# Score matmuls cut into 32 weight columns, other planned transfer lengths, and loads of a DRAM tile placed behind its last store

## The chip, the core and the metric

One NeuronCore of a Trainium2 chip runs the whole program. The metric is the device time of one execution in microseconds. The engines are PE (TensorE: matmuls and transposes; its weight loads, PEld, run beside them), DVE (VectorE), ACT (ScalarE), POOL (GpSimd) and SP (SyncE, which here only issues DMAs). Each engine runs its own instructions in the order in which the program emitted them, and waits on semaphores for the others.

## The reference

Three stages in a row, all in float32. B = 8 batches, H = 8 heads, S = 576 tokens, D = 64, 32 packed queries per head.

```python
def sm_attn(qq, kk, vv):                      # softmax attention, scale 1/sqrt(64)
    s = scale * np.matmul(qq, kk.transpose(0, 1, 3, 2))
    ...
    return np.matmul(a, vv)
p_packed = sm_attn(p, k, v)                   # 32 packed rows per head
x = sm_attn(q, p_packed, p_packed)            # every token against the 32 rows
x = x.transpose(0, 2, 1, 3).reshape(4608, 512)

expert_idx = np.argmax(xn @ en.T / tau, 1)    # 8 experts, one for each token
out[mask] = gate_w[mask, None] * (np.maximum(x[mask] @ w1[e], 0) @ w2[e])

a = x @ w_a;  b = x @ w_b                     # x is now the output of the experts
return a * b @ w_out                          # 512 -> 1536 -> 512
```

## The kernel before, in words

**Attention** (up to about 210 us). `prep(b)` loads p, k (two halves of four heads, 0.59 MB each) and v (1.18 MB; two halves for batch 0) of one batch, transposes k, computes the scores of the 32 packed rows and multiplies them with v. `query(u)` treats one of 18 units of 256 tokens: 128 partitions of two tokens each. It loads q (line 423), transposes it (433), and `s2_mm` (447) multiplies it, for each head, with the packed rows ppT of the token's batch. What follows in `rest` is a softmax on DVE and ACT, a transpose (501), the product with the packed rows (512) and the store of x to a DRAM tile (537).

In `s2_mm` the 128 columns of a unit are the weight side of the matmul. `pieces(sg, most)` cuts them: a piece is 32, 64 or 128 columns, at most `most`, starts at a multiple of its own size and stays inside one batch. Batches are 288 of these columns long, so four units (2, 6, 11 and 15) are cut between two batches at column 32 or 96. With `most` = 64 they fall into pieces of 32, 32 and 64 columns, and all others into two pieces of 64. A unit has two groups of four heads: so there are 8 groups of 4 x 3 matmuls ("mixed" below) and 28 groups of 4 x 2 ("even" below). The trace shows each float32 matmul as two instructions.

**Routing.** As soon as 25 of the 36 tiles of x are there, DVE ranks the tokens by expert (the function of line 784 and the steps recorded at line 685), and POOL gathers the rows of x for the first experts' slots while the last units of attention still run.

**Experts** (about 213 to 661 us): 16 slots of 288 tokens. A slot has four groups of 24 `up` matmuls and four of 24 `dn` matmuls (lines 1038 to 1040). Its weights are loaded by SP (line 1178) into raw tiles, and ACT and DVE split each into a high and a low part (1338, 1340). ACT issues two stores for each slot (line 1267) that put the transposed result into a DRAM tile, `x2T`. Beside the slots, SP loads, and DVE and ACT convert, the weights of the last stage (1069 to 1099), and `before` (line 1583 ff.) prepares the first pair of token halves for it: nine loads of 0.39 MB from `x2T` (line 1596), sums on DVE (1568), and a split on ACT (1575) and DVE (1578).

**Last stage** (to the end): a loop of matmuls for w_a, w_b and w_out.

**What sets the order.** All of this is given as operations to a planner, `Sched`. An operation has a planned length on the engines that may do it, a priority, the operations that it needs, and the buffers that it takes and frees. `run` picks, again and again, the operation that can start first by the plan (of those within 0.05 us of it the one of lowest priority), and emits it. So the planned lengths and priorities set only the order of the instructions on each engine; the chip waits for real semaphores. DMAs planned on "D" are issued by SP in that order. A load of `x2T` on the chip waits for every store to `x2T` that was emitted before it, whichever rows it reads.

Of the kernel before, what the change touches and what calls it, by code (L numbers as in the profile page):

```python
# [18 lines left out]
B, H, S, D, NP, E = 8, 8, 576, 64, 32, 8  # L19
# [52 lines left out]
class Sched:  # L72
# [14 lines left out]
        self.sizes, self.taken = sizes, {p: [] for p in sizes}  # L87
        self.ops = []

    def op(self, engs, fn, deps=(), prio=0.0, take=(), free=(), lat=None, bias={}, start=0.0, after=None):  # L90


        o = self.Op()
        o.engs, o.fn, o.deps, o.prio, o.take, o.free = engs, fn, [d for d in deps if d], prio, take, free
        o.lat, o.end, o.bias, o.start, o.after = self.LAT if lat is None else lat, None, bias, start, after
        for b in free:
            b.need += 1
        self.ops.append(o)
        return o

    def run(self, most=None, **clock):


        todo = list(self.ops)
        while todo:
            cand = []
            for n, o in enumerate(todo[:most]):
                if any(d.end is None for d in o.deps) or o.after and o.after.end is None:
                    continue
                ready, ok = {None: o.start}, True  # L110
                for i, b in enumerate(o.take):
                    t = self.taken[b.pool]
                    at = len(t) - self.sizes[b.pool] + sum(b2.pool == b.pool for b2 in o.take[:i])
                    if at >= 0:
                        old = t[at]
                        ok = ok and old.need == 0
                        ready[None] = max(ready.get(None, 0.0), old.at + self.LAT)
                if not ok:
                    continue
                best = None  # L120
                for e, dur in o.engs.items():
                    at = max([clock.get(e, 0.0), ready.get(None, 0.0)]
                             + [d.end + (self.SAME if d.eng == e and d.lat <= self.LAT else d.lat) for d in o.deps])
                    key = at + dur + o.bias.get(e, 0.0)
                    if best is None or key < best[0]:
                        best = (key, at, dur, e)
                cand.append((best[1:], n, o))
            assert cand, "no operation can go"
            t0 = min(x[0][0] for x in cand)
            (at, dur, e), n, o = min((x for x in cand if x[0][0] <= t0 + self.EPS),  # L130
                                     key=lambda x: (x[2].prio, x[0][0], x[1]))
            todo.pop(n)
            o.eng, o.end = e, at + dur
            if e != "none":
                clock[e] = o.end
            for b in o.take:
                self.taken[b.pool].append(b)
            for b in o.free:
                b.need -= 1
                b.at = max(b.at, o.end)  # L140
            o.fn(e)
        return clock


def attention(ctx, tc, c, q, k, v, p, x_dram, consts, more):
# [28 lines left out]
    op, Buf = S_.op, Sched.Buf  # L174
# [26 lines left out]
    def pieces(sg, most):  # L201

        for b, _, n, o in sg:
            end = o + n
            while o < end:
                m = max(x for x in (32, 64, 128) if x <= most and o % x == 0 and o + x <= end)
                yield b, o, m
                o += m
# [5 lines left out]
    ppT_ops, ppx_ops = {}, {}  # L214

    def prep(b):
        ahead = AHEAD
        lo, hi = (first[b - 1] - ahead, first[b] - ahead) if b else (-8.0, -1.0)
        at = lambda f: lo + (hi - lo) * f
# [6 lines left out]
        def load(n, x, h0, n_h):  # L226
            def f(e):
                if n == "k":
                    tile_("k", ("k", b, h0 // 4), [CW, 4, CI, D])
                    out = T_["k", b, h0 // 4]  # L230
                else:
                    if h0 == 0:
                        tile_(n, (n, b), [CW, H, CI, D])
                    out = T_[n, b][:, h0:h0 + n_h]
                nc.sync.dma_start(out=out, in_=x[b, h0:h0 + n_h].rearrange("h (p i) d -> p h i d", i=CI))
            return f

        o_p = op({"D": 0.2}, load_p, prio=at(-1.0), take=[bp], lat=2.0)
        o_k, o_v = [], []
        for n, x, l, pr, n_h in (("k", k, o_k, -1.0, 4), ("v", v, o_v, -0.6, 4 if b == 0 else H)):  # L240
            for h in range(0, H, n_h):
                l += [op({"D": 3.3 * n_h / H}, load(n, x, h, n_h), deps=l[-1:], prio=at(pr) + 0.01 * h,
                         take=[bk[h // 4]] if n == "k" else [] if h else [bv], lat=2.0)] * n_h


# [13 lines left out]
        o = op({"T": 0.44}, pT_mm, deps=[o_p], prio=at(0), take=[t, bpT], free=[bp])  # L259
# [16 lines left out]
        for h in range(H):  # L276
            t = Buf("tr")
            bkT.append(Buf(f"kT{h}"))
            o = op({"T": 0.25}, kT_mm(h), deps=[o_k[h]], prio=at(0.03 * h), take=[t, bkT[h]], free=[bk[h // 4]])
            o_kT.append(op({"A": 0.3, "V": 0.36}, kT_ev(h), deps=[o], prio=at(0.03 * h), free=[t]))  # L280

        for g in range(2):
# [97 lines left out]
            f = lambda x, g=g: at(x + 0.17 * g)  # L380
            be, beT, bs = Buf("e"), Buf("eT"), Buf("sm")
            evs = []
            for h in range(2):
                t = Buf("tr")
                o = op({"T": 0.56}, s1_mm(h), deps=[o_pT] + o_kT[4 * g:4 * g + 4], prio=f(0.2), take=[t] if h else [t, be],
                       free=[bpT] + bkT[4 * g:4 * g + 4])
                evs.append(op({"A": 0.3, "V": 0.36}, s1_ev(h), deps=[o] + evs, prio=f(0.2),
                              free=[t]))
            o = op({"V": 0.86}, mx, deps=evs, prio=f(0.3))
# [25 lines left out]
    def query(u):  # L415

        sg = segs(u)
        bs = [b for (b, _, _, _) in sg]

        def load(e):  # L420
            tile_("q", ("q", u), [128, H, 2 * D])
            for (b, col, n, o) in sg:
                nc.sync.dma_start(out=T_["q", u][o:o + n],
                                  in_=q[b, :, col:col + 2 * n, :].rearrange("h (p r) d -> p h (r d)", r=2))


        def qT_mm(g):
            def f(e):
                ps = psum("tr", ("qTp", u, g))
                if g == 0:  # L430
                    tile_("qT", ("qT", u), [128, H, 128])
                for j in range(4):
                    nc.tensor.transpose(ps[:, j * 128:(j + 1) * 128], T_["q", u][:, 4 * g + j, :], c.ident)
            return f

        def qT_ev(g):
            return lambda e: copy(e, T_["qT", u][:, 4 * g:4 * g + 4],
                                  T_["qTp", u, g].rearrange("p (i q) -> p i q", i=4))

        def s2_mm(g):  # L440
            def f(e):
                if g == 0:
                    psum("sm", ("s2", u))
                for j in range(4):
                    h = 4 * g + j
                    for b, o, n in pieces(sg, 64):
                        nc.tensor.matmul(
                            T_["s2", u][o:o + n, h * 64:h * 64 + 64], lhsT=T_["qT", u][:, h, o:o + n],
                            rhs=T_["ppT", b, g][:, j].rearrange("p r k -> p (r k)"), start=True, stop=True)
            return f  # L450

        B_ = {n: Buf(n) for n in ("q", "qT", "sm")}
        o = op({"D": 1.46}, load, prio=2 * u - 3.5, take=[B_["q"]], lat=2.0)
        qs, ss = [], []
        for g in range(2):
            tr = Buf("tr")
            o_q = op({"T": 0.44}, qT_mm(g), deps=[o] + qs, prio=2 * u - QA, take=[tr] + ([] if g else [B_["qT"]]),
                     free=[B_["q"]])
            qs.append(op({"A": 0.47, "V": 0.6}, qT_ev(g), deps=[o_q], prio=2 * u - QA, free=[tr]))
        for g in range(2):  # L460
            ss.append(op({"T": 0.61}, s2_mm(g), deps=[qs[g]] + [d for b in bs for d in ppT_ops[b, g]] + ss,
                         prio=2 * u, take=[] if g else [B_["sm"]],
                         free=[B_["qT"]] + [T_["bppT", b, g] for b in bs]))
        for r in range(2):
            rest(u, r, sg, bs, ss, B_["sm"])

    def rest(u, r, sg, bs, ss, sm):
# [92 lines left out]
        o_sq = op({"A": 0.62}, sq, deps=[o], prio=f(1.5), take=[B_["sq"]], free=[B_["sq"], B_["xs"]])  # L560
        o_d = op({"P": 0.17}, dots, deps=[o], prio=f(1.5), free=[B_["xs"]])
        o_r = op({"P": 0.55}, root, deps=[o_sq], prio=f(1.5))
        o_s = op({"D": 0.73}, store, deps=[o], prio=f(1.0), free=[B_["xs"]], lat=2.0)
        x_ops[t] = (o_r, o_d, o_s)

    for b in range(B):
# [918 lines left out]
class Moe2:  # L1485
# [96 lines left out]
    def before(self, S, pool, conv, stores, y, n, routed, raw):  # L1582


        D, op, Buf, HB = self.nc.sync, S.op, S.Buf, self.HB
        ys = [y[s, i] for s in range(-(-2 * HB // SLOT)) for i in (1, 3)]
        q_at, o_q, b_q = {}, {}, {}

        def load(key, p, tag, bufs):
            b_q[key], st = Buf(tag), {}  # L1590
            q_at[key] = st

            def f(e):
                st["t"] = pool.tile([128, 2, HB], F32, tag=tag, name="xq64", bufs=bufs)
                r0, t0 = key[0] * 256, key[1] * HB
                D.dma_start(out=st["t"], in_=self.x2T[r0:r0 + 256, t0:t0 + HB].rearrange("(k p) t -> p k t", p=128))

            o_q[key] = op({"D": 1.1}, f, deps=ys, prio=p, take=[b_q[key]], lat=2.0)

        p = n - 2.6  # L1600
        order = dict((name, parts) for name, _, parts in self.ORDER)
# [512 lines left out]
```

## Time and profile before

| | us |
|---|---|
| median of 3 runs | 1511.3 (1503.77 to 1513.59) |
| the profiled execution | 1511.94 |
| its span, first to last instruction | 1510.2 |
| PE busy | 1467.4 (97% of the span) |
| DVE, ACT, POOL busy | 946.4, 741.2, 169.9 |
| DMA | 276.15 MB, 183 GB/s over the span |

The profiled execution took 0.64 us longer than the median, and 1.7 us of it lie outside its span. Busy time of PE is the union of its matmuls, with modelled ends; PEclk is the TensorE clock that was granted, as a share of full speed.

### The profile page before, as it was taken

What the parts mean: (1) busy time and instruction counts of PE and PEld (TensorE: products, weight loads), DVE (VectorE), ACT (ScalarE), POOL (GpSimd) and SP (SyncE); (2) the same over time, 40 slices, a digit from 0 to 9 for tenths busy, and PEclk for the clock granted to TensorE, in tenths of its full rate; (3) what the DMA queues carried; (4) which work ended last, traced back from release to release, by engine and by line L of the source; (5) the groups of instructions that cost most, each with busy time, mean ns of one, the idle gap of its engine ahead of it and who ended that gap; (6) DMA issues with size and microseconds to landing.
All of it is one profiled execution on the core that took longest, in us unless ns stands there. A gap on an engine that the chain in (4) does not pass through costs nothing.

```text
span 1510.2 us, 27918 instructions
## 1 busy us (share of the span) xinstructions
PE 1467.4 (97%) x10257; PEld 1341.2 (89%) x10257; DVE 946.4 (63%) x1954; ACT 741.2 (49%) x1530; POOL 169.9 (11%) x274
## 2 busy tenths in 40 slices
PE   6999988999999999999999999999999999999997
PEld 4667668999999999989999999999999999999996
DVE  3566789998899886638886535544464365343442
ACT  4677766466666665535555333433443253333332
POOL 1333350120111101100002000100010010001001
PEclk9999999999999999999999999999999999999998
DMA  9788461284777866247777555755665575556551
GB/s 239 198 221 219 125 195 46 63 239 137 230 210 234 256 188 199 81 144 244 272 255 253 161 161 158 241 159 156 204 204 160 157 240 162 161 153 207 162 154 63
DMA packets 199121, 276.15 MB, mean 183 GB/s; under 512 B 16664, under 2 KB 116248, under 8 KB 198976
## 3 DMA queue, kind: packets, MB, share of 16 engines
q1 hardware_dynamic: 183776, 244.76, 54.4%
q0 software_dynamic: 6336, 20.06, 4.0%
q10 hardware_dynamic: 8864, 9.46, 1.8%
q8 instruction: 84, 1.38, 0.4%
q14 instruction: 61, 0.50, 0.1%
HBM read 256.39 MB, written 59.77 MB: 209 GB/s over the span
## 4 chain that ended last, share of the span: by engine, by line
issue 37%; PE 17%; POOL 1%; DMA 1%; ACT 0%; POOLq 0%; ACTq 0%
PE o L1929 2%; PE o L1928 2%; PE o L1930 2%; PE pa L1040 2%; PE pb L1040 2%; PE pb L1039 2%; PE pa L1039 2%; PE pb L1038 2%; PE pa L1038 2%; POOL out_dram L1952 1%; DMA out_dram<-osb,idxu 1%; ACT osb L1947 0%; ACT s L1815 0%; POOL mark L1951 0%; ACT xq L1726 0%
## 5 line engine op out<-in xcount | busy, mean ns | idle before, releaser
L1679 DVE TENSOR_TENSOR s<-s,s 128x384 f32<-128x384 f32 x324 | 176.5, 555 | 325.3 <-ACT s L1815 323.0
L1038 PE MATMUL pa<-xq,wq 128*128 128x384 f32 x504 | 169.9, 337 | 3.4 <-PEq L1468 1.8
L1038 PE MATMUL pb<-xq,wq 128*128 128x384 f32 x504 | 170.2, 338 | 1.0 <-DVE s L1679 0.7
L1928 PE MATMUL o<-oh,gh 128*128 128x512 f32 x432 | 170.3, 394 | 0.8 <-ACT osb L1947 0.8
L1040 PE MATMUL pa<-xq,wq 128*128 128x384 f32 x504 | 170.6, 339 | 0.0
L1039 PE MATMUL pb<-xq,wq 128*128 128x384 f32 x504 | 170.4, 338 | 0.0
L1040 PE MATMUL pb<-xq,wq 128*128 128x384 f32 x504 | 170.4, 338 | 0.0
L1929 PE MATMUL o<-ol,gh 128*128 128x512 f32 x432 | 170.4, 394 | 0.0
L1930 PE MATMUL o<-oh,gl 128*128 128x512 f32 x432 | 170.3, 394 | 0.0
L1039 PE MATMUL pa<-xq,wq 128*128 128x384 f32 x504 | 170.2, 338 | 0.0
L1815 ACT COPY s<-pa 128x384 f32<-128x384 f32 x180 | 86.6, 481 | 152.8 <-PE pa L1040 152.6
L1038 PE MATMUL up<-xh,w1h 128*128 128x288 f32 x512 | 153.3, 299 | 4.6 <-DVE hl L1239 4.0
L1815 ACT COPY s<-pb 128x384 f32<-128x384 f32 x180 | 86.7, 482 | 143.4 <-PE pb L1040 143.3
L1038 PE MATMUL dn<-hh,w2h 128*128 128x288 f32 x512 | 155.0, 303 | 0.0
L1039 PE MATMUL up<-xl,w1h 128*128 128x288 f32 x512 | 152.3, 297 | 0.3 <-DVE xl L1313 0.3
L1040 PE MATMUL up<-xh,w1l 128*128 128x288 f32 x512 | 151.8, 296 | 0.0
L1039 PE MATMUL dn<-hl,w2h 128*128 128x288 f32 x512 | 151.7, 296 | 0.0
L1040 PE MATMUL dn<-hh,w2l 128*128 128x288 f32 x512 | 151.5, 296 | 0.0
L1952 POOL DMA_INDIRECT out_dram<-osb,idxu x30 | 32.3, 1078 | 683.7 <-ACT osb L1947 683.3
L1038 PEld LDWEIGHTS pa<-xq,wq 128*128 128x128 f32 x504 | 95.0, 188 | 12.0 <-DVE s L1679 2.2
L1038 PEld LDWEIGHTS pb<-xq,wq 128*128 128x128 f32 x504 | 94.9, 188 | 10.5 <-DVE s L1679 1.0
L1039 PEld LDWEIGHTS pb<-xq,wq 128*128 128x128 f32 x504 | 94.8, 188 | 8.4
(265 smaller groups left out, 3143.5 us busy)
## 6 DMA issues: line engine op xcount, KB each, us to landing
wq<-ws SPq DMA_DIRECT2D x420, 256.0 KB
raw<-in_moe_w_dram SPq DMA_DIRECT2D x128, 512.0 KB
ws<-wq SPq DMA_DIRECT2D x84, 256.0 KB
k<-in_k_dram SPq DMA_DIRECT2D x16, 576.0 KB
x_dram<-xs SPq DMA_DIRECT2D x36, 256.0 KB
x2T<-y ACTq DMA_DIRECT2D x32, 288.0 KB
v<-in_v_dram SPq DMA_DIRECT2D x7, 1152.0 KB
xr<-x2T SPq DMA_DIRECT2D x20, 384.0 KB
```

The lines of the kernel that those rows point to most:

```text
L1038: nc.tensor.matmul(ps, lhsT=wh, rhs=xh, start=start, stop=False, **kw)
L1039: nc.tensor.matmul(ps, lhsT=wh, rhs=xl, start=False, stop=False, **kw)
L1040: nc.tensor.matmul(ps, lhsT=wl, rhs=xh, start=False, stop=stop, **kw)
L1679: VT = lambda out, a, b, o: V.tensor_tensor(out=out, in0=a, in1=b, op=o)
L1815: A.copy(out=T[n, key], in_=ps[n, names_bank[key]])
L1928: nc.tensor.matmul(a, lhsT=gh[:, h, s], rhs=wh, start=first, stop=False)
L1929: nc.tensor.matmul(a, lhsT=gh[:, h, s], rhs=wl, start=False, stop=False)
L1930: nc.tensor.matmul(a, lhsT=gl[:, h, s], rhs=wh, start=False, stop=last)
L1952: i = nc.gpsimd.indirect_dma_start(out=self.out, out_offset=IOA(ap=c.idxu[:, q:q + 1], axis=0), in_=st["o"], in_offset=None)
```

## The change

It does three things. `s2_mm` cuts the weight columns into pieces of at most 32 instead of 64, for all 18 units: 16 matmuls for each group of four heads, instead of 12 or 8, with 0.58 instead of 0.61 us in the plan. The planned lengths of attention's transfers go up by about 30% (k and v 3.3 to 4.2 for eight heads, q 1.46 to 1.9, the store of x .73 to .95), and the priorities of the k and v loads of a batch go up, that is later: from -1.0 and -0.6 to -0.75 and -0.45 of a batch's stretch. And the planner gets a rule: an operation can be given others that it comes `behind`, and then starts in the plan no sooner than `land` after the end of those of them that are placed already. The nine loads of `x2T` come behind the stores of odd index, two of a slot's four, with land = 7.0, and their planned length goes from 1.1 to 1.5. No work is added but the cut, and none is taken away; line numbers in the changed file are 4 higher after line 130 and 5 higher in `before`.

```diff
-    def op(self, engs, fn, deps=(), prio=0.0, take=(), free=(), lat=None, bias={}, start=0.0, after=None):
+    def op(self, engs, fn, deps=(), prio=0.0, take=(), free=(), lat=None, bias={}, start=0.0, after=None,
+           behind=(), land=0.0):
...
+        o.behind, o.land = behind, land
...
                 if not ok:
                     continue
+                ready[None] = max([ready[None]] + [d.end + o.land for d in o.behind if d.end is not None])
...
-        for n, x, l, pr, n_h in (("k", k, o_k, -1.0, 4), ("v", v, o_v, -0.6, 4 if b == 0 else H)):
+        for n, x, l, pr, n_h in (("k", k, o_k, -0.75, 4), ("v", v, o_v, -0.45, 4 if b == 0 else H)):
             for h in range(0, H, n_h):
-                l += [op({"D": 3.3 * n_h / H}, load(n, x, h, n_h), deps=l[-1:], prio=at(pr) + 0.01 * h,
+                l += [op({"D": 4.2 * n_h / H}, load(n, x, h, n_h), deps=l[-1:], prio=at(pr) + 0.01 * h,
...
-                    for b, o, n in pieces(sg, 64):
+                    for b, o, n in pieces(sg, 32):
...
-        o = op({"D": 1.46}, load, prio=2 * u - 3.5, take=[B_["q"]], lat=2.0)
+        o = op({"D": 1.9}, load, prio=2 * u - 3.5, take=[B_["q"]], lat=2.0)
...
-            ss.append(op({"T": 0.61}, s2_mm(g), ...
+            ss.append(op({"T": 0.58}, s2_mm(g), ...
...
-        o_s = op({"D": 0.73}, store, deps=[o], prio=f(1.0), free=[B_["xs"]], lat=2.0)
+        o_s = op({"D": 0.95}, store, deps=[o], prio=f(1.0), free=[B_["xs"]], lat=2.0)
...
         ys = [y[s, i] for s in range(-(-2 * HB // SLOT)) for i in (1, 3)]
+        out = [o for (_, i), o in y.items() if i % 2]
...
-            o_q[key] = op({"D": 1.1}, f, deps=ys, prio=p, take=[b_q[key]], lat=2.0)
+            o_q[key] = op({"D": 1.5}, f, deps=ys, prio=p, take=[b_q[key]], lat=2.0, behind=out, land=7.0)
```

Since the planner sees other lengths, the order of the whole of attention moves. Three places follow.

The first is PE's order at unit 2, which lies across batches 0 and 1 (ppT_190 and ppT_191 are their packed rows, sm the scores in PSUM). Before:

```order
L512 MATMUL x<-ppx_549,aT 128x264
L447 MATMUL sm<-ppT_190,qT 32x64
L447 MATMUL sm<-ppT_191,qT 32x64
L447 MATMUL sm<-ppT_191,qT 64x64
L447 MATMUL sm<-ppT_190,qT 32x64
```

And of the change:

```order
L451 MATMUL sm<-ppT_190,qT 32x64
L451 MATMUL sm<-ppT_191,qT 32x64 x3
L451 MATMUL sm<-ppT_190,qT 32x64
L451 MATMUL sm<-ppT_191,qT 32x64 x3
L516 MATMUL x<-ppx_421,aT 128x264
```

The piece of 64 columns became two of 32, and each head now has four pieces of one shape.

The second place is PE's order in the first expert slots, at the second ranking (O is the one-hot of the experts, xt a PSUM tile; ACT copies what the matmul with the ones has written there, before the matmul with the triangle `low` comes). Before:

```order
L1040 MATMUL up_3726<-xh,w1l_93 128x288
L784 LDWEIGHTS ones
L784 MATMUL xt_3729<-O,ones 128x288
L1212 MATMUL xt_3730<-ident,xg_81 128x96
L1212 MATMUL xt_3730<-ident,xg_82 128x96
L1212 MATMUL xt_3730<-ident,xg_83 128x96
L784 LDWEIGHTS low
L784 MATMUL xt_3729<-O,low 128x288
L1038 MATMUL dn_3727<-hh_3715,w2h_3707 128x288
```

And of the change:

```order
L788 LDWEIGHTS ones
L788 MATMUL xt_3985<-O,ones 128x288
L1216 MATMUL xt_3986<-ident,xg_81 128x96
L1216 MATMUL xt_3986<-ident,xg_82 128x96
L1216 MATMUL xt_3986<-ident,xg_83 128x96
L1042 MATMUL up_3982<-xh,w1h_92 128x288
L1043 MATMUL up_3982<-xl,w1h_92 128x288
L1044 MATMUL up_3982<-xh,w1l_93 128x288
```

A whole group of 24 `up` matmuls, up_3982, stands now between the two matmuls of the ranking; `low` comes after it.

The third place is SP's order near the end of the experts, with the loads of `x2T` (xq) between the loads of the experts' weights (raw). Before:

```order
L1178 DMA raw_3703<-in_moe_w_dram 128x8x128
L1596 DMA xq_8052<-x2T 128x2x384
L1178 ISA
L1178 DMA raw_3704<-in_moe_w_dram 128x8x128
L1178 ISA
L1178 DMA raw_3705<-in_moe_w_dram 128x8x128
L1178 ISA
L1178 DMA raw_3706<-in_moe_w_dram 128x8x128
L1099 DMA wb_63<-ca 128x512
L1596 DMA xq_8158<-x2T 128x2x384
L1596 DMA xq_8186<-x2T 128x2x384
```

And of the change:

```order
L1182 DMA raw_3961<-in_moe_w_dram 128x8x128
L1182 ISA
L1182 DMA raw_3962<-in_moe_w_dram 128x8x128
L1601 DMA xq_8779<-x2T 128x2x384
L1601 DMA xq_8782<-x2T 128x2x384
L1601 DMA xq_8826<-x2T 128x2x384
L1601 DMA xq_8856<-x2T 128x2x384
L1601 DMA xq_8901<-x2T 128x2x384
L1601 DMA xq_9055<-x2T 128x2x384
L1472 COMPARE_AND_BRANCH
```

Six of the nine loads now stand behind the last load of expert weights, with nothing but a branch behind them.

## Rows read from the trace of the kernel before

**Rows 1.** The page: busy time of PE, and the granted clock in 40 slices.

```profile
PE 1467.4 (97%) x10257; PEld 1341.2 (89%) x10257; DVE 946.4 (63%) x1954; ACT 741.2 (49%) x1530; POOL 169.9 (11%) x274
PEclk9999999999999999999999999999999999999998
```

**Rows 2.** Windows of 20 us: busy us (count) per engine, PEclk, DMA share, GB/s.

```profile
20.00:40.00 20.00, 14.78 (x252) 10.11 (x245) 9.24 (x30) 8.00 (x21) 2.40 (x4) 0.91 1.14 249
80.00:100.00 20.00, 20.00 (x301) 14.35 (x299) 14.97 (x53) 14.61 (x41) 5.62 (x12) 1.00 0.92 235
160.00:180.00 20.00, 19.98 (x325) 14.54 (x314) 16.82 (x66) 15.88 (x45) 6.99 (x14) 1.00 0.35 107
180.00:200.00 20.00, 17.07 (x242) 12.01 (x240) 19.32 (x62) 13.34 (x33) 10.16 (x15) 0.94 0.52 160
200.00:220.00 20.00, 17.83 (x106) 12.22 (x102) 15.11 (x44) 13.29 (x35) 14.08 (x20) 0.98 0.72 208
220.00:240.00 20.00, 16.08 (x110) 15.48 (x109) 17.64 (x36) 14.10 (x22) 0.00 (x0) 0.91 0.44 118
240.00:260.00 20.00, 20.00 (x152) 19.85 (x151) 19.10 (x57) 11.91 (x19) 2.93 (x3) 1.00 0.19 60
580.00:600.00 20.00, 16.77 (x109) 16.54 (x108) 16.85 (x22) 13.33 (x20) 0.00 (x0) 0.83 0.50 161
```

**Rows 3.** Groups of instructions, PE: busy us, mean ns | idle us before, releaser.

```profile
L447 PE MATMUL sm<-ppT,qT 128*64 128x64 f32 (+1 forms) x640 | 35.6, 232 | 1.2 <-DVE acc L997 1.2
```

**Rows 4.** Timeline of PE in attention: start us, us, what, count [idle before <-releaser].

```profile
138.63 2.02 PE L447 MATMUL sm<-ppT,qT 128*32 128x64 f32 x24
...
162.54 0.54 PE L339 MATMUL sm<-v,eT 96*32 96x64 f32 x24
...
164.61 0.69 PE L447 MATMUL sm<-ppT,qT 128*64 128x64 f32 x16
...
169.51 1.18 PE L289 MATMUL tr<-kT,pT 128*32 128x288 f32 x16
...
182.60 0.95 PE L339 MATMUL sm<-v,eT 96*32 96x64 f32 x48
...
184.02 2.05 PE L447 MATMUL sm<-ppT,qT 128*64 128x64 f32 x24
...
194.98 1.15 PE L447 MATMUL sm<-ppT,qT 128*64 128x64 f32 x32 [1.18 <-DVE acc L997]
```

**Rows 5.** Waits of PE, 0 to 240 us: us in total, times, longest.

```profile
PE tr L433 <- DMA q<-in_q_dram: 3.3, 1, 3.3
PE xt L784 <- ACT rt L788: 3.1, 1, 3.1
PE tr L268 <- DMA k<-in_k_dram: 2.3, 2, 1.5
...
PE sm L447 <- DVE acc L997: 1.2, 1, 1.2
```

**Rows 6.** Timeline of DVE at the end of the first ranking.

```profile
194.89 0.40 DVE L474 TENSOR_REDUCE mx<-sm 128x8 f32<-128x256 f32 x1
```

**Rows 7.** Timeline of SP (issues) around the second load of `x2T`.

```profile
567.50 0.39 SPq L1178 DMA_DIRECT2D raw<-in_moe_w_dram  x1
574.72 0.39 SPq L1596 DMA_DIRECT2D xq<-x2T  x1
```

**Rows 8.** Waits of SP, 540 to 661 us: us in total, times, longest.

```profile
SPq L1596 <- DMA x2T<-y: 7.0, 2, 6.8
```

**Rows 9.** Timeline of PE, slot 13: the wait at its third group of `up`.

```profile
584.38 0.61 PE L1038 MATMUL up<-xh,w1h 128*128 128x288 f32 x1 [3.23 <-DVE hl L1239]
```

**Rows 10.** Timeline of ACT: the first store of three slots in a row.

```profile
541.68 0.38 ACTq L1267 DMA_DIRECT2D x2T<-y  x1
...
568.32 0.38 ACTq L1267 DMA_DIRECT2D x2T<-y  x1
...
600.97 0.46 ACTq L1267 DMA_DIRECT2D x2T<-y  x1
```

More of the change, by code (lines that the diff above doesn't have):

```diff
@@ L460, in query @@
         for g in range(2):
-            ss.append(op({"T": 0.61}, s2_mm(g), deps=[qs[g]] + [d for b in bs for d in ppT_ops[b, g]] + ss,
+            ss.append(op({"T": 0.58}, s2_mm(g), deps=[qs[g]] + [d for b in bs for d in ppT_ops[b, g]] + ss,
                          prio=2 * u, take=[] if g else [B_["sm"]],
```

## The prediction

> **What bounds the kernel now.** I read the page first: PE is busy for 1467.4 of 1510.2 us, at an almost full clock [rows 1]. So PE sets the time, and a change can win in two ways only: by making PE's own work shorter, or by closing its gaps, 42.8 us in all. I then read the windows of 20 us, to see where the gaps are [rows 2]. Between 60 and 180 us PE has none worth naming: two windows stand for the six, at 20.00 and 19.98. PE falls short in four places that the change touches: the start (20 to 40 us), the end of attention and the first expert slots (180 to 240), and the window from 580. In three of them the granted clock is 0.91 or less too, so each gap is paid twice. DMA is not the bound in attention on the whole: its share is 1.14 from 20 to 40 us (over one engine set because packets overlap), but 0.92 at 80 and 0.35 at 160 [rows 2]. DVE is nearly full from 180 to 200 (19.32): that is the first ranking.
>
> Then, for each edit, I went to the rows of the line it touches.
>
> **The score matmuls.** Line 447 issues 640 instructions, 35.6 us of PE in all [rows 3]. An even group (16 instructions, two 64-column pieces abreast) takes 0.69 us; a mixed group (24) takes 2.05, or 2.02 [rows 4]. So a mixed group costs three times an even one, with half as many instructions more. Another line shows that this need not be so: line 339 runs 32-column pieces throughout, and 24 of those take 0.54, 48 take 0.95 [rows 4], so 24 more cost 0.41, or 0.017 for one. The rows show a cost of mixing the two shapes, not of small pieces.
> After the change every group has 16 matmuls, 32 instructions, all of 32 columns. By line 339: 0.54 + 8 x 0.017 = 0.68 us.
> - Mixed groups: 2.05 - 0.68 = 1.37 each, eight of them. Six lie before 167 us, where PE has no gaps, so all of it counts: 6 x 1.37 = **-8.2**. Two lie at 184.0 and four us later, beside DVE's ranking, where PE is idle for 2.9 us of 20 [rows 2]; PE waits there for DVE's `acc` anyway [rows 5]. I take 0; the bound is -2.7.
> - Even groups: 0.69 against 0.68, 28 of them: 0. Line 339 has only 96 rows of weights; with 128 rows and 32 columns there is line 289, 16 instructions of 288 columns in 1.18 us [rows 4]. Scaled from 288 to 64 columns a step is 0.074 x 64/288 = 0.016 for one, again the 0.017. The price in the other direction is in the last rival.
>
> The Trainium skill says otherwise for the even groups: "TensorEngine Tiling (Array Packing)", section "Instruction Overhead", gives each matmul about 60 cycles whatever its size, and advises not to take a tiling factor from a dimension that is already small. By that, 16 more instructions in each of 28 even groups would cost 16 x 25 ns = 0.4 us each, 11 us in all, an estimate from that page at 2.4 GHz. The trace has 17 ns for one 32-column instruction, four being abreast, so the row is against it.
>
> **The loads of x2T.** SP issued the load of 574.72 after 7.2 us in which it issued nothing [rows 7], and of its waits 6.8 us go to a store of x2T that had not landed [rows 8]. Three loads of expert weights stood behind it on SP, as the order shows; their splits came late, and behind those DVE's `hl`: PE waited 3.23 us for it [rows 9], and the clock of the window was 0.83 [rows 2], which over 20 us is 3.4 us more. The stores say what the slot lost: 541.68 to 568.32 is 26.64, 568.32 to 600.97 is 32.65 [rows 10], so **-6.0** if the wait goes. In the new order six of the nine loads stand behind the last weight load: what they delay on SP is nothing of the experts. Where one still stands between weight loads, the store of 568.32 bounds what a landing takes: no more than 574.72 - 568.32 = 6.4 us [rows 7, 10], and the plan now leaves 7.0. What the late loads now delay is the work of DVE and ACT on the first pair itself, which stands in order between the splits of the last two slots. No row shows how much room there is; I take it that there is enough, and the first rival is that there is not. Bounds: -3 (a small wait stays and the clock drops again) to -6.6 (3.23 + 3.4).
>
> **The second ranking.** PE waits 3.1 us for ACT's copy between the two matmuls of the ranking [rows 5]. Now 24 `up` matmuls stand between them: at 20.00 us for 152 [rows 2] they take 3.2 us, so they cover it. I take **-3.0**. The clock loss of that window, 0.09 x 20 = 1.8, may go as well: bounds 0 (the wait only moves to the next `dn`, whose `hl` is later) to -4.9.
>
> **The start.** PE waits 3.3 us for the second unit's q [rows 5], and the window's clock costs 1.8. By the shapes in SP's new order the bytes ahead of that q are the same, 5.9 MB, but more of batch 0's work stands ahead of its transposes on PE. I take **-1.0**. Bounds: -5 (both go) to +3: the second half of batch 1's k now has 5.4 MB ahead of it on SP instead of 3.7, at 249 GB/s 6.8 us later, of which I leave half uncovered at the worst.
>
> **New waits.** Two stores of x now stand ahead of the next q and k loads on SP, and a store that waits for its copy holds up the loads behind it. Every k and v comes later by plan. The waits for k were 1.5 us at the longest [rows 5]: I add one of 1.3. The index of the first ranking comes four operations later on DVE, each up to 0.40 us in that stretch [rows 6] and overlapping a little, so 0.3: 1.2, with the gathers and the first `up` behind it. Together **+2.5**, bounds 0 and +6 (the 1.2 and three waits for k).
>
> The transfer lengths and priorities do nothing on the chip but to move the order: their cost is in the last two parts.
>
> **Sum:** -8.2 - 6.0 - 3.0 - 1.0 + 2.5 = -15.7 on the profiled 1511.94 (0.64 above the median) gives 1496.2 from there, and 1495.6 from the median. I say **1496**. What a measurement of this kernel can tell from no change is about 1%, 15 us: faster means below 1496.2. The forecast stands on that line.
>
> **The rivals.**
> - *The wait for x2T only moves.* DVE and ACT take their work in order; the sum and split of the first pair wait for loads that now come late, and if one stands ahead of a split of slot 14 or 15, PE waits as before. For it: both engines' orders put work of the first pair ahead of such splits, and loads that used to be spread over two slots now come in one row. Against: six loads with no weight behind them, and a plan that allows each landing its 6.4 us. It gives back the 6.0: 1502. Chance 0.15.
> - *Attention gives nothing.* The first expert slot waits for the first ranking, and that for DVE. If DVE, or a later k or v, and not PE sets when the 25th tile is done, the 8.2 becomes idle time in front of the first `up`. For it: DVE at 19.32 from 180, 16.82 from 160. Against: DVE is at 14.97 of 20 at 80 us, with PE full, so it follows PE until the ranking begins. 1496.2 + 8.2 = 1504. Chance 0.20.
> - *All of it counts.* The two late mixed groups pay too (-2.7), the second ranking gives its clock back (-1.8), and the new waits are covered (-2.5): 1496.2 - 7.0 = 1489. Chance 0.10.
> - *Small pieces run only two abreast,* the other side. Then a group of 32 instructions costs what two even groups back to back do, 1.15 us [rows 4]. The even groups lose 28 x 0.46 = 12.9, the six mixed ones win only 6 x 0.9 = 5.4, the ranking starts later so that the gain there is lost, and the rest stays: 1511.94 + 12.9 - 5.4 - 6.0 + 2.5 = 1516. Each microsecond more for a group costs 34 (28 even, 6 mixed), and without the 4.0 of the second ranking and the start the gain is 11.7: so it decides from 11.7/34 = 0.34 us more for a group. Against it stand lines 339 and 289. Chance 0.05. The page named above points this way; by its 0.4 us it would be near this time.
>
> The forecast itself has 0.50, with 1488 to 1501 as its own range: the bounds of the second ranking, the start and the new waits half used.
>
> **How the numbers follow.** The range of 1486 to 1508 takes the forecast's range, most of the third rival, and the first two with their spread of 3 or 4 us; left out are the last rival and the tails, under 2 in 10. Faster by over 1%: a little over half of the forecast's 0.50, the 0.10 of the third, and 0.06 of the first two: 0.43. Slower by over 1%, above 1526: the last rival's upper part and a starved start together, 0.05. Within 1%: the rest, 0.52.
>
> **What would show it.** All 36 groups of the scores at about 0.68 us, with 1152 instructions in 25 us in place of 640 in 35.6. No wait of SP for x2T before the last load of weights, and the stores of slots 12 to 15 all 26.6 apart. No wait of 3.1 at the second ranking. The first `up`, now at 213 us, some 8 us earlier. Groups of 1.15 would show the last rival; a first `up` at 213 with mixed groups at 0.68 the second; a slot of 30 us or more near the end the first. The sum is wrong most easily where it is least read from rows: a new wait for k or v in attention, since the whole order of its loads has moved.

## The result, and the profile after

The changed kernel takes 1496.26 us (median of 6 runs, 1492.01 to 1498.04), the one before 1510.85 (6 runs beside it): a ratio of 0.9907, with a 95% interval of 0.9889 to 0.9925. The prediction was 1496. It was 0.3 us off, and that is luck in part: three of its terms were off by nearly 4 us each, one of them the other way, and smaller ones made up most of the rest.

The page of the profiled execution (1498.04 us, span 1496.3), busy time and clock, to be read against [rows 1]:

```profile
PE 1454.9 (97%) x10769; PEld 1331.9 (89%) x10769; DVE 946.6 (63%) x1953; ACT 742.2 (50%) x1530; POOL 168.5 (11%) x275
PEclk9999999999999999999999999999999999999998
```

PE has 512 instructions more and is busy 12.5 us less, 11.1 of it in the scores. 13.9 us of span have gone, and PE's idle time fell by only 1.4, from 42.8 to 41.4 us. That is a balance: gaps that closed at the start came up again behind it, as the windows below show. The scores, as a group of instructions (busy us, mean ns | idle before):

```profile
L451 PE MATMUL sm<-ppT,qT 128*32 128x64 f32 x1152 | 24.5, 227 | 1.1 <-ACT as L489 0.7 <-issue 0.3
```

They fell from 35.6 us [rows 3] to 24.5. One group of them, at unit 2, in the timeline of PE:

```profile
42.29 0.65 PE L451 MATMUL sm<-ppT,qT 128*32 128x64 f32 x32
```

A mixed group took 2.05 before [rows 4]. Now 31 of the 36 groups take 0.63 to 0.67, mixed and even alike; the others are the first one, which has a gap inside, and two pairs that run back to back. The windows of 20 us (columns as in [rows 2]):

```profile
20.00:40.00 20.00, 17.71 (x367) 12.76 (x366) 11.68 (x39) 12.95 (x34) 4.90 (x10) 1.00 1.06 253
...
160.00:180.00 20.00, 17.03 (x366) 12.64 (x365) 19.19 (x68) 15.09 (x41) 9.22 (x16) 1.00 0.56 185
180.00:200.00 20.00, 15.48 (x131) 8.54 (x130) 17.02 (x47) 14.16 (x35) 12.32 (x18) 0.87 0.43 127
200.00:220.00 20.00, 18.95 (x123) 18.24 (x121) 14.01 (x36) 12.24 (x21) 3.57 (x5) 0.87 0.75 202
220.00:240.00 20.00, 18.30 (x136) 17.70 (x135) 18.90 (x55) 14.12 (x23) 2.76 (x3) 1.00 0.19 60
240.00:260.00 20.00, 18.02 (x135) 17.21 (x135) 19.62 (x49) 8.46 (x13) 0.00 (x0) 1.00 0.04 15
...
560.00:580.00 20.00, 17.91 (x123) 17.67 (x123) 13.90 (x23) 11.81 (x20) 1.68 (x2) 0.91 0.81 223
580.00:600.00 20.00, 20.00 (x156) 20.00 (x156) 12.90 (x18) 10.99 (x18) 2.89 (x3) 1.00 0.21 68
```

Three things are to be seen. The start is fuller (17.71 of 20 for 14.78, and the clock stays full). The gaps at the end of attention and in the first slots are all there, and deeper: from 160 to 260 PE lacks 12.2 us; before, from 174 to 274, where about the same work stood, it lacked 9.9. And the window of the wait for x2T, now 560 to 580 since all is earlier, still lacks 2.1 us and some clock.

The window at 560 decides what became of the term of 6.0 us. First SP's timeline there, to be read against [rows 7]:

```profile
557.12 0.39 SPq L1182 DMA_DIRECT2D raw<-in_moe_w_dram  x1
557.55 1.59 SPq L1557 DMA_DIRECT2D wq<-wa  x2
561.10 0.38 SPq L1182 DMA_DIRECT2D raw<-in_moe_w_dram  x1
```

DVE, at the first instruction that uses wq:

```profile
566.96 0.43 DVE L1572 TENSOR_TENSOR wsum<-wq 128x256 f32<-128x256 f32 x1 [4.75 <-DMA wq<-wa]
```

PE, at the place of [rows 9]:

```profile
572.59 0.40 PE L1042 MATMUL up<-xh,w1h 128*128 128x288 f32 x1 [2.09 <-DVE hl L1243]
```

And ACT's first store of slots 11, 12 and 13, as in [rows 10]:

```profile
531.03 0.38 ACTq L1271 DMA_DIRECT2D x2T<-y  x1
...
557.66 0.41 ACTq L1271 DMA_DIRECT2D x2T<-y  x1
...
588.17 0.38 ACTq L1271 DMA_DIRECT2D x2T<-y  x1
```

SP no longer waits for x2T: the loads of wq, weights of the last stage, stand there instead. They were issued without delay, but took until 566.96 to be of use, and DVE stood still for them 4.75 us with the splits of the expert weights behind. PE then waited 2.09 us for `hl`, the same instruction that it waited for in [rows 9]. Slot 13, from the first store of slot 12 to its own, takes 588.17 - 557.66 = 30.51 us, not 26.6; before it was 32.65 [rows 10]. A wait was replaced, not removed.

What it replaced was a wait of the same kind. DVE at that place in the trace before:

```profile
578.02 0.96 DVE L1568 TENSOR_TENSOR xq<-xq,xq 128x768 f32<-128x768 f32 x1 [4.83 <-DMA xq<-x2T]
```

And ACT:

```profile
579.02 0.83 ACT L1575 CAST xq<-xq 128x768 fp32r<-128x768 f32 x1 [5.55 <-DVE xq L1568]
```

The two engines that make the splits stood still for the sum of the first pair, with splits behind it. No split there waits for a load of weights.

The same points of the program, found in both traces (us, and the difference). "Again" is a second execution of the changed kernel on another occasion:

| point | before | after | again |
|---|---|---|---|
| 169th of 224 instructions x<-ppx ends | 175.81 | -14.12 | -12.71 |
| first `up` starts | 212.96 | -12.04 | -10.55 |
| first store of slot 1 | 269.76 | -11.50 | -10.32 |
| first store of slot 3 | 326.55 | -10.66 | -9.93 |
| first store of slot 12 | 568.32 | -10.66 | -9.93 |
| first store of slot 13 | 600.97 | -12.80 | -13.70 |
| 14th matmul of the last stage | 665.35 | -14.64 | -15.68 |
| end of the span | 1510.21 | -13.88 | -14.09 |

So 14 us are won by 176 us, 3.5 of them are lost again in the first slots, 2.1 (3.8 the second time) come from slot 13, and about 2 from the start of the last stage. That last part is no effect of the change: kernels below that leave this place as before show it too, against the one execution of before, which had a slow stretch there, behind 1.8 us in which PE was idle. The granted clock was 0.59 for 4.2 us, so most of it at the lower level of 1.2 GHz:

```profile
661.00:665.20 4.20, 3.75 (x13) 3.78 (x14) 0.76 (x2) 0.48 (x1) 0.09 (x1) 0.59 1.05 310
```

### The profile page after: what moved, and what is told of

It reads as the page before. It is cut to its first block, busy times and chain, and to the rows that moved or that the text cites. A ratio compares the mean times of both kernels' runs of the same rounds, so it can differ in the third digit from the quotient of the medians.

```text
span 1496.3 us, 28939 instructions
## 1 busy us (share of the span) xinstructions
PE 1454.9 (97%) x10769; PEld 1331.9 (89%) x10769; DVE 946.6 (63%) x1953; ACT 742.2 (50%) x1530; POOL 168.5 (11%) x275
## 4 chain that ended last, share of the span: by engine, by line
issue 37%; PE 17%; POOL 2%; DMA 0%; ACT 0%; POOLq 0%; ACTq 0%
PE o L1934 2%; PE o L1933 2%; PE o L1935 2%; PE pa L1044 2%; PE pb L1043 2%; PE pb L1044 2%; PE pa L1043 2%; PE pb L1042 2%; PE pa L1042 2%; POOL out_dram L1957 2%; DMA out_dram<-osb,idxu 0%; POOL mark L1956 0%; ACT oend L1952 0%; ACT osb L1952 0%; POOLq L1957 0%
```

## The experiments

All ratios are to the kernel before, run on the same chip. The rounds of runs were on different chips, so kernels of different rounds are compared by their ratios. One execution is not the next: at the first point of the table, two kernels below whose attention is that of before, instruction by instruction, stand at -1.82 and +0.68. So a landmark of one trace is good to about 2 us, a length inside one slot to 1 or 2.

**The cut alone.** On the kernel before:

```diff
-                    for b, o, n in pieces(sg, 64):
+                    for b, o, n in pieces(sg, 32):
```

> The kernel before with the cut into 32 columns alone; planned lengths, priorities and order as before. Theory (the cut pays where PE has no gaps): all groups at 0.65 us, the last x matmul before the first ranking some 9 us earlier (six mixed groups of 1.40 saved and 0.04 in each even one), of which the DVE-bound first expert slots give back 0 to 3.5; the wait of 6.0 for x2T stays. Total 5.5 to 9.5 us less than before. Rival (the arrival of k and v and the ranking set the pace of attention): the first expert slot is not earlier, total within 2 us of before.

1500.16 us, ratio 0.9939 (0.9919 to 0.9960): 9.2 us less. A mixed group in its timeline of PE:

```profile
46.22 0.65 PE L447 MATMUL sm<-ppT,qT 128*32 128x64 f32 x32
```

The first point of the table is at -11.2, the first store of slot 3 at -11.0, slot 13 at 31.42 us. This is the theory: the cut brings nearly two thirds of the whole, and the first slots, in the old order, give none of it back.

**The cost of mixing.** On the kernel before, all 32-column matmuls of a group first, then all of 64; nothing else moves:

```diff
+                for w in (32, 64):
                     for j in range(4):
...
+                            if n != w:
+                                continue
```

> The kernel before, with the matmuls of a group put out by size: in a mixed group the eight of 32 columns first and then the four of 64, one switch instead of eight; the order of everything else is the same. Theory (a mixed group is dear because each switch between 32 and 64 columns costs about 0.15 us): mixed groups fall from 2.05 to about 1.2 us, even groups stay at 0.69. Rival (it is dear because the pieces of 64 run alone, or by the number of matmuls): mixed groups stay at 1.8 us or more.

One execution was timed, 1503.71 us. Two mixed groups in its timeline of PE:

```profile
49.32 1.25 PE L450 MATMUL sm<-ppT,qT 128*32 128x64 f32 x24
...
50.90 1.25 PE L450 MATMUL sm<-ppT,qT 128*32 128x64 f32 x24
```

The same 24 instructions in another order take 1.25 us, not 2.05. So of the 1.40 us that the change saves in a mixed group, 0.80 is the switching between the two shapes: one switch in the group instead of seven, 0.13 us for each that went. The other 0.60 is not taken apart by any run. That a 64-column piece has no second one beside it in a mixed unit would fit, and is not shown.

**The planned lengths and priorities alone.**

```diff
-        for n, x, l, pr, n_h in (("k", k, o_k, -1.0, 4), ("v", v, o_v, -0.6, 4 if b == 0 else H)):
+        for n, x, l, pr, n_h in (("k", k, o_k, -0.75, 4), ("v", v, o_v, -0.45, 4 if b == 0 else H)):
-                l += [op({"D": 3.3 * n_h / H}, load(n, x, h, n_h), ...
+                l += [op({"D": 4.2 * n_h / H}, load(n, x, h, n_h), ...
-        o = op({"D": 1.46}, load, prio=2 * u - 3.5, ...
+        o = op({"D": 1.9}, load, prio=2 * u - 3.5, ...
-        o_s = op({"D": 0.73}, store, ...
+        o_s = op({"D": 0.95}, store, ...
```

> The kernel before with the planned transfer lengths of attention and the later priorities of k and v alone. Theory (the order of the first loads closes gaps of the start): x matmuls from 60 us on are 4 to 5 us earlier, of which some is lost at the first expert slots; total 2 to 5 us less than before. Rival (the start was won by the shorter scores, or is given back by later waits for k and v): total within 1.5 us of before, or more than it.

1506.41 us, ratio 0.9981 (0.9965 to 0.9997): 2.9 us less. The window of the start:

```profile
20.00:40.00 20.00, 19.34 (x336) 14.05 (x335) 11.78 (x38) 14.36 (x39) 4.88 (x9) 1.00 1.07 249
```

PE does 19.34 us where it did 14.78 [rows 2], with the same DMA rate of 249 GB/s: the bytes come in an order that PE can use. The 41st instruction x<-ppx ends 5.3 us earlier, with the scores as they were; the new order of loads is worth this much at the start, less the 2 us by which executions differ. The first `up` is 4.4 us earlier, the first stores of slots 1 and 3 are 7.4 and 7.1: here, against the expectation, the first slots lose nothing.

**The placing alone.**

```diff
+        out = [o for (_, i), o in y.items() if i % 2]
-            o_q[key] = op({"D": 1.1}, f, deps=ys, prio=p, take=[b_q[key]], lat=2.0)
+            o_q[key] = op({"D": 1.5}, f, deps=ys, prio=p, take=[b_q[key]], lat=2.0, behind=out, land=7.0)
```

> The kernel before with the placing of the x2T loads behind the last store alone. Theory (the wait is replaced by a smaller one: the loads of wq for the last stage now stand where the x2T loads stood, and DVE's first sum of them holds up the splits behind it): slot 13 takes about 30.5 us from first store to first store, where before it was 32.65 and an undisturbed one is 26.6; total 2 to 4.5 us less than before. Rival (the wait goes altogether and what the changed kernel still loses there comes from its other edits): slot 13 at 26.6, total 6 us less.

1510.31 us, ratio 0.9997 (0.9979 to 1.0016): nothing that can be told. Slot 13 takes 598.99 - 566.13 = 32.86 us. Neither the theory's 30.5 nor the rival's 26.6: the new wait is as long as the old one. SP's timeline at that place:

```profile
565.75 2.90 SPq L1556 DMA_DIRECT2D wq<-wa  x2
```

DVE's:

```profile
577.84 0.43 DVE L1571 TENSOR_TENSOR wsum<-wq 128x256 f32<-128x256 f32 x1 [6.33 <-DMA wq<-wa]
```

And PE's, at the third group of `up`:

```profile
583.47 0.61 PE L1041 MATMUL up<-xh,w1h 128*128 128x288 f32 x1 [4.50 <-DVE hl L1242]
```

It is the chain seen in the profile after, and longer: 12.1 us from the issue of wq to its use, where the plan allows 1.46 + 2.0. In the changed kernel it was 9.4.

**The new wait taken away.** In the changed kernel, the planned latency of that one load:

```diff
-        o_w = op({"D": 1.46}, load_w, deps=deps, prio=p, take=[bw], lat=2.0)
+        o_w = op({"D": 1.46}, load_w, deps=deps, prio=p, take=[bw], lat=8.0)
```

> The changed kernel with one number changed: the planned latency of the first load of wq for the last stage is 8.0 instead of 2.0, so that DVE's first sum of it stands two weight splits later; SP's order is the same. Theory (that sum, waiting for a load that takes 8 us to land, is the new wait of slot 13): slot 13 falls from 30.5 to 26.6 to 27.5 us, total 3 to 4 us less than the changed kernel, about 1492.5. Rival (the splits come late because SP issues their loads late): slot 13 stays near 30.5, total the same as the changed kernel's.

1493.12 us, ratio 0.9897 (0.9863 to 0.9931): by the ratios 1.5 us less than the changed kernel, under the 3 to 4 expected, with a wide interval. SP issues in the same order; DVE's first sum of wq stands two splits later. DVE waits there for at most 1.5 us, and no longer for wq; a row of its timeline:

```profile
564.85 1.23 DVE L1344 TENSOR_TENSOR w2l<-raw,w2h 128x1024 fp32r<-128x1024 f32 x1 [1.42 <-ACT w2h L1342]
```

ACT's first store of slots 12 and 13:

```profile
556.42 0.41 ACTq L1271 DMA_DIRECT2D x2T<-y  x1
...
583.44 0.38 ACTq L1271 DMA_DIRECT2D x2T<-y  x1
```

Slot 13 takes 27.02 us. Within the slot, the wait for wq was the rest of the lost term.

**Both on the kernel before.** The placing and the latency of 8.0, nothing else of the change:

> The kernel before with the placing of the x2T loads, and the planned latency of the first wq load at 8.0. Theory (the wait at slot 13 has two causes in a row, and both have to go): slot 13 at 26.6 to 27.2 us and total 5 to 6.5 us less than before, where the placing alone gave nothing. Rival (what the later wq brought depends on the order of attention in the changed kernel): total within 2 us of before.

1505.58 us, ratio 0.9976 (0.9956 to 0.9996). Slot 13 takes 594.43 - 567.06 = 27.37 us, 5.3 less than before. The runs say 3.6 us less (0.6 to 6.6), under the 5 to 6.5 expected, with an interval that holds them. Most of the 6.0 of the prediction is there to be had in the slot, but not by the placing alone. The latency of 8.0 without the placing was not run.

**All but the placing.** Cut, lengths and priorities on the kernel before (0.61 left as the scores' planned length):

> The changed kernel without the placing of the x2T loads (cut, planned lengths and priorities as changed, 0.61 left as the planned length of the scores). Theory (the placing alone is worth nothing, since its new wait for wq takes the place of the old one): total within 3 us of the changed kernel, slot 13 at 31 to 33 us in place of 30.5. Rival (it is worth the 6 us of the prediction): total 5 us or more above the changed kernel.

1497.37 us, ratio 0.9925 (0.9895 to 0.9955), against 0.9907 for the changed kernel: 2.7 us more, which these intervals do not tell from nothing. Slot 13 takes 586.06 - 554.75 = 31.31 us, 0.8 more than in the changed kernel. As far as these runs can tell, the change would have been worth nearly the same without its placing.

**Where the first slots lose 3.5 us.** In all thirteen traces the first store of slot 1 follows SP's first load of slot 0's second weights by 54.7 to 57.8 us, in twelve of them by 56.5 at most. That load stands on SP behind the last six stores of x. SP's timeline there, before:

```profile
202.35 10.95 SPq L537 DMA_DIRECT2D x_dram<-xs  x6
213.57 1.21 SPq L1178 DMA_DIRECT2D raw<-in_moe_w_dram  x2
```

And after:

```profile
187.23 15.21 SPq L541 DMA_DIRECT2D x_dram<-xs  x6
202.71 1.09 SPq L1182 DMA_DIRECT2D raw<-in_moe_w_dram  x2
```

The 217th of the 224 instructions x<-ppx ends at 208.46 and 194.29: the loads come 5.1 us after it before, 8.4 after. The stores wait there for ACT's and DVE's copies of x. That these stand behind more of other work in the new order is not counted here.

Two kernels narrow down where this comes from. The kernel with all but the placing, which plans the scores at 0.61 us instead of 0.58, has these loads 4.0 us after the 217th, and loses 1.1 us up to slot 3; the lengths and priorities alone have them after 4.3 and lose nothing. The placing alone leaves the order of attention as it was. That leaves the 0.58, a planned length and no work, for the order in which the loads come late; no run has it alone. How much that costs is less sure: the four executions with that order have the loads after 7.2 to 8.4 us, and lose 1.0 to 3.5 us.

So, on the kernel with the latency of 8.0, ACT issues these six stores:

```diff
-            nc.sync.dma_start(
+            (nc.scalar if t >= 30 else nc.sync).dma_start(
                 out=x_dram[t * 128:(t + 1) * 128, :]...
-        o_s = op({"D": 0.95}, store, ...
+        o_s = op({"A": 0.4} if t >= 30 else {"D": 0.95}, store, ...
```

> The changed kernel with the wq latency of 8.0, and the stores of the last six tiles of x issued by ACT in place of SP, so that SP's loads of the first slot's second weights do not stand behind them. Theory (the first expert slots are held by these loads: in six kernels so far the first store of slot 1 came 55.0 to 56.2 us after the first of them): the first of them is issued 3 to 8 us earlier, the first store of slot 1 comes earlier by 2 to 5 us, total 1488 to 1491. Rival (DVE, at 19.6 of 20 us from 240 on, holds them by its own work): the loads go earlier, the first store of slot 1 stays, total within 1.5 us of 1493.

SP's loads in its timeline:

```profile
197.10 4.80 SPq L1182 DMA_DIRECT2D raw<-in_moe_w_dram  x4
```

ACT's first store of slot 1:

```profile
253.24 0.38 ACTq L1271 DMA_DIRECT2D x2T<-y  x1
```

The load goes 5.4 us earlier than in the kernel it is built on (202.5), and the first store of slot 1 4.6 earlier (257.85); 1.9 us of both were there at the first point of the table, as executions differ. In a second pair of executions, those of the last two kernels below, the three figures are 7.5, 5.7 and 2.5. So some 3 us of the first slots hang on where these stores stand, and not on the amount of DVE's work, which is the same. The planner's order of DVE and ACT also moved from 188 us on, and no run holds that apart. But the time is 1493.87 us, ratio 0.9889 (0.9871 to 0.9908): the theory's 1488 to 1491 is missed. Of the 4.6 us 2.1 are left at the last stage; slots 12 and 13 take 55.7 us together, with the planner's new order of x2T loads there, and the last stage is 2.3 us longer (2.2 in the second pair), for a reason that stays open.

**Three kernels side by side,** the changed one and the last two versions, on one chip.

> The changed kernel once more, beside the two that follow and on the same chip. Theory and rival alike: 0.990 to 0.992 of before, near 1496.

> The changed kernel with the wq latency of 8.0 once more. Theory (the 3.4 us that slot 13 loses less reach the end): 0.987 to 0.989 of before, 2 to 5 us less than the changed kernel beside it. Rival (they are lost in the last stage, which differs by 2 us from one execution to the next in all kernels so far): within 1.5 us of the changed kernel.

> The kernel with the six stores of x on ACT and the wq latency of 8.0 once more. Theory (the 4.6 us won at slot 1 are there in each execution, half of them lost again by slot 13): 0.986 to 0.988 of before. Rival (all of them are lost again): the same as the kernel with the wq latency alone, within 1.5 us.

| | median us | ratio to before | interval |
|---|---|---|---|
| changed kernel | 1494.77 | 0.9905 | 0.9884 to 0.9927 |
| with the wq latency of 8.0 | 1492.69 | 0.9889 | 0.9868 to 0.9911 |
| and six x stores on ACT | 1491.79 | 0.9886 | 0.9864 to 0.9907 |

The version with the latency of 8.0 is 2.1 us faster than the changed kernel by these medians, and 1.5 by the ratios of the first rounds (0.9897 and 0.9907); the intervals of the ratios overlap, so the order is likely, not certain. The stores on ACT add nothing that can be told (0.9 us here, 1.2 by the ratios of the first rounds, 0.9889 and 0.9897): the rival.

Slot 13 is 26.99 us in the second kernel, and 28.88 in the changed one, where it was 30.51 the first time. The waits were alike: DVE's for wq 4.75 and 4.64 us, PE's for `hl` 2.09 and 1.98. What differs is the granted clock behind them. The first execution of the changed kernel:

```profile
575.00:580.00 5.00, 5.00 (x32) 5.00 (x32) 3.68 (x7) 2.71 (x6) 0.00 (x0) 0.79 0.36 102
```

And the second:

```profile
575.00:580.00 5.00, 5.00 (x41) 5.00 (x40) 4.47 (x8) 3.43 (x7) 0.00 (x0) 1.00 0.45 130
```

The same gap was paid twice in one execution and once in the other.

## Why the prediction was right, and which steps were wrong

| step | predicted | measured, one pair of traces |
|---|---|---|
| six mixed groups | -8.2 | -8.4 (6 x 1.40) |
| two late mixed groups | 0 | 0 |
| even groups, 24 before 176 us | 0 | -1.0 (0.04 each) |
| start | -1.0 | -4.7 (what is left of -14.12) |
| second ranking and new waits | -0.5 | +3.5 |
| x2T | -6.0 | -2.1 |
| last stage | not named | -1.1 |
| sum | -15.7 | -13.8 |

**The score matmuls** were right, in mechanism and size: 0.68 forecast from line 339, 0.65 found. The cut alone brings 9.2 us, and sorting the pieces shows that more than half of the saving in a mixed group is the switching. The last rival, pieces that run two abreast, is refuted by 32 instructions in 0.65 us; and what the Trainium skill says under "TensorEngine Tiling (Array Packing)", section "Instruction Overhead", read as a cost for each matmul, would by the prediction's estimate have added 0.4 us to each even group. That does not hold against the trace here: an even group got 0.04 us shorter with 16 more instructions. The two late groups are free, as said: in the kernel with the cut alone the stretch from the 169th to the 217th x<-ppx is 33.7 us, before it was 32.7 (31.4 to 33.5 in three other kernels with the order of before).

**The start** was mis-sized. I took a third of a wait that I could see, and left the clock to the bound. The new order closes most gaps up to 40 us: the bound of -5 was nearer than the value. Of the -4.7, 1 to 2 us may be the execution of before (the second execution of the changed kernel gives -3.3).

**The second ranking and the new waits** failed in sum, +3.5 for -0.5. The wait of 3.1 us at the ranking did fall, to 1.1:

```profile
PE xt L788 <- ACT rt L792: 1.1, 1, 1.1
PE tr L272 <- DMA k<-in_k_dram: 1.0, 1, 1.0
```

But it was not worth its length: the first stores of slots 1 to 3 hang on when SP gets past the last stores of x, and PE just waits elsewhere. And the new wait is not for k, which I priced (its waits fell, from 2.3 to 1.0): it is on SP, whose last stores of x wait for ACT's and DVE's copies while the experts' weights stand behind them. I had named a store that holds up the loads behind it, and looked for it in front of loads of q and k only.

**The loads of x2T** are the step that failed outright. "If the wait goes" was right: from 540 to 650 us SP waits for x2T no more. The reading of what the wait did was not. I put PE's wait down to weight loads that came late behind it on SP; the rows of DVE and ACT show both standing still for the sum of the first pair, 4.83 and 5.55 us, with the splits behind that. So the room on DVE that I took for granted was what had to be asked for. I asked what was late next among the loads that were moved, and not what moved up into their place: the wq loads went one slot ahead (issued at the first store of slot 12, before at that of slot 13), and DVE's sum of them stood before the splits of slot 13. The first rival had the mechanism (DVE takes its work in order, and a late load in front of a split stops PE) and the wrong load. The placing alone is worth nothing that can be told (0.9997), and with the wait for wq gone 5.3 us in the slot. Even the -2.1 of the table is not all the placing's: in four kernels that leave these loads as before, slot 13 takes 31.25 to 32.31 us, in the one trace of before 32.65.

The forecast came out at 1496.26 for 1496 because the start and the scores won 4.9 us more than said, the first slots and x2T 7.9 less, and the last stage, by the slow stretch of before, gave 1.1. That leaves 1.9 too little in the pair of traces, and the traced execution of the changed kernel is itself 1.8 us above its median. That the two meet within 0.3 us is luck.

## What to carry to other kernels

Cut matmuls that share an output into one shape, or at least put those of one shape together: alternating cost 0.80 us in a group of 12, the smaller shape nothing. When a transfer is late, look for the instruction that stands still for it before pricing what is queued behind it. When it is moved off a queue's critical place, read what the planner puts there next, and how long that takes on the chip against its planned latency; a load planned at 3.5 us that takes 9 to 12 holds an in-order engine just as the old one did. And read a gain from where the next stage starts: 14 us won in attention were 10.7 at the fourth slot, since the order on another queue set part of that start.

## What the runs showed that was not expected

- The load of wq, 256 KB twice, took 9.4 us from issue to use in one order and 12.1 in another, where the plan has 3.5; the DMA share was 0.98 from 555 to 565 us, in the first.
- Six switches fewer between matmuls of 32 and 64 columns saved 0.80 us in a group of 12.
- A planned length of 0.58 instead of 0.61 us for the scores, the only other difference but the placing, goes with loads that come 3 to 4 us later behind the end of attention. No run has it alone.
- Executions of one program differ by up to 3.7 us by the 41st instruction x<-ppx (63.84 and 67.54 us in two executions of the kernel with the latency of 8.0), but by 0.8 us at most in the last stage. In slot 13 two executions of the changed kernel differ by 1.6 us, nearly all of it the clock behind one and the same gap.
